# Dynamic convolution, layer norm and feed-forward on one core: hidden-layer products of 64 channels taken in pairs, another order of the first loads, and a new plan

## The chip, the core and the metric

The kernel runs on one core of a Trainium2 chip. A core has five engines with a queue each: PE (TensorE, matmuls), DVE (VectorE), ACT (ScalarE), POOL (GpSimd) and SP (SyncE, which here only issues DMAs). Each runs its own instructions in order and waits on semaphores for the others. PE reads its operands from SBUF and writes to PSUM; 16 DMA engines move data between HBM and SBUF and within SBUF. The metric is the device time of one execution in microseconds, as the median of several runs.

## The reference

Eight sequences of 4224 tokens with 192 channels. Each token is replaced by a weighted sum of itself and the six tokens before it, the weights being a softmax over 7 values for each of 8 heads of 24 channels; then follow a layer norm and a feed-forward network of 192 to 768 to 192 with a ReLU and a residual.

```python
def _attn_ref(x, weight_gen):
    w = np.exp(weight_gen - np.max(weight_gen, axis=-1, keepdims=True))
    w = w / (np.sum(w, axis=-1, keepdims=True) + 1e-09)
    x_pad = np.concatenate([np.zeros((B, pad, D)), x], axis=1)
    idx = np.arange(S)[:, None] + np.arange(K)[None, :]
    x_unf = x_pad[:, idx, :].reshape(B, S, K, H, group)
    return np.einsum('bshk,bskhg->bshg', w, x_unf).reshape(B, S, D)

def _moe_ref(x, g_ln, w_ch1, w_ch2):
    mu = np.mean(x, axis=-1, keepdims=True)
    var = np.mean((x - mu) ** 2, axis=-1, keepdims=True)
    xn = (x - mu) / np.sqrt(var + 1e-06) * g_ln
    return x + np.maximum(xn @ w_ch1, 0.0) @ w_ch2
```

x, weight_gen and g_ln come as float32, w_ch1 (W1) and w_ch2 (W2) as float64.

## The kernel before

**Tiling.** The 33,792 tokens are spread over 128 partitions, so that each partition holds a run of 264 neighbouring tokens ("columns", C = 264). PARTS cuts the 264 columns into parts of 4, 8 or 12 columns for the layer norm, CHUNK = 6 (or 4) columns is the piece of a convolution, and NT = 4 columns (512 tokens) is a group of the feed-forward network; there are 66 groups.

**Stages of a column.** `load_w` (L295) and `load_x` (L280) issue the loads on SP. x lies in a ring of RING = 36 columns with PAD = 6 columns ahead of it, which repeat the last columns of the round before, so that a chunk at the ring's start finds its six older tokens; every round they are loaded from HBM again (L290), and at the very start a load of the neighbouring partition's last columns fills them (L287). `softmax` (L304) works with DVE, POOL and ACT. `conv` (L351) makes seven products per chunk on DVE, in four instructions (L383), into `y` and the `pr` buffers; two accumulating DMAs within SBUF (L389) and four adds on POOL (L386) sum them. For the first EARLY = 1 chunks POOL makes one add of two pairs (L399) and DVE the other four (L386). `norm` (L417) sums and squares on ACT (L427, L432), takes the root on ACT and DVE (L455 to L466), scales y to `xh` (L478), splits it into a high and a low fp16 part `hl` (high on ACT, L485, low on POOL, L487), and SP transposes `hl` by DMA into `xT` (L491). For each column the 384 values are high 0 to 191, then low 0 to 191, which gives three blocks of 128 rows: high 0 to 127; high 128 to 191 over low 0 to 63; low 64 to 191.

**The products.** W1 and W2 too are split into fp16 high and low parts. `products` (L495) computes the hidden layer of a group in three units of 256 hidden channels each (u = 0, 1, 2). A unit is ten matmuls of 512 columns (L506): for each half of 128 hidden channels, W1 high with all three blocks, and W1 low with the first two. Of the second block W1 low needs only the 64 high rows; the other 64 rows add a product of two low parts. The unit's result, two banks of PSUM called `ph` (a pool of two such buffers), is read by ACT (ReLU to `hh`, L515) and then by DVE (the remainder to `hlo`, L517). `output` (L526) makes 18 matmuls of 192 columns per column of tokens (L538 to L540) into `po`, DVE scales and adds the residual (L551), and SP stores a finished chunk.

**Weights.** `load_weights` (L577) issues the loads of W1 (two, 768 and 384 KB) and g on ACT's queue and W2's on SP's. `from_double` (L590) turns float64 bits into float32 on DVE and ACT; `weights` (L649) then scales, splits and, by small DMAs within SBUF (`shift`, L686), brings pieces of the split W1 to other partitions. The steps carry names: "a" and "c" are the two pieces of W1, "s1" their scaling, "c2" and "s2" the same of W2.

**The order.** No engine's order is written out. Every operation is registered with `op` (L64) with its engine, a cost in ns and a "want", a due time in units of a column; `Plan.order` (L89) then simulates the engines with these costs and picks, among the operations that can start within AHEAD ns of the earliest, the one with the smallest want; buffers are assigned on the way. The tables WANT, W_WANT and FIRST (L30 to L35) hold the due times of each step relative to its column. The order so found is fixed before the kernel runs.

## Time and profile before

| | |
|---|---|
| runs, median (lowest to highest of 3) | 910.77 us (909.26 to 911.03) |
| the profiled execution, device time | 914.2 us |
| its span, first to last instruction | 912.4 us |
| products on PE, first to last | 57.65 / 907.5 us |
| mean granted PE clock | 0.994 |
| moved by DMA | 145.12 MB |

The profile was taken of one execution. "Busy" adds up the time in which an engine has an instruction in work; matmuls are pipelined, so their durations overlap and a step is read from one start to the next. A group of instructions is named by line, engine, operation and tiles, with its count, its busy time and the mean of one in ns. An idle stretch is put down to the instruction that ended last among those waited for. PEld is the loading of weights, PEq, SPq and the like are the engines' sequencers with the issue of DMAs.

### The profile page before, as it was taken

The numbers are of one execution on the slowest core, as the hardware profiler recorded it, in microseconds if no ns is written. First come the engines' busy times: TensorE is split into PE (matmuls) and PEld (weight loads), VectorE is DVE, ScalarE is ACT, GpSimd is POOL, SyncE is SP. The second block draws the span as 40 slices with busy tenths as digits, with TensorE's granted clock in tenths as the row PEclk, the third lists the DMA queues.
The fourth block names the chain that finished last, engine by engine and source line by source line (L and its number), as shares of the span: only waits on it lengthen the run. The fifth ranks groups of instructions, "written<-read, shape, count | busy, mean of one in ns | idle before, by whom it ended". The sixth has DMA issues, their size and how long they took to land. (4 is left out here: it accounts for less than half of the span.)

```text
span 912.4 us, 17537 instructions
## 1 busy us (share of the span) xinstructions
PE 831.8 (91%) x6736; PEld 587.2 (64%) x6736; DVE 788.4 (86%) x837; ACT 667.1 (73%) x1766; POOL 689.9 (76%) x398
## 2 busy tenths in 40 slices
PE   0029899999999999999999999999999999999997
PEld 0015577666767677776666667777677777677776
DVE  4999899999999999889798898998989989884342
...
GB/s 229 157 178 155 142 195 180 192 180 116 201 222 165 186 149 169 200 146 197 148 154 179 147 205 157 171 201 136 203 163 156 190 151 145 140 111 91 75 30 52
DMA packets 138667, 145.12 MB, mean 159 GB/s; under 512 B 107551, under 2 KB 108831, under 8 KB 138583
## 3 DMA queue, kind: packets, MB, share of 16 engines
...
q8 instruction: 52, 0.85, 0.4%
...
## 5 line engine op out<-in xcount | busy, mean ns | idle before, releaser
L386 POOL TENSOR_TENSOR y<-y,pr 128x1152 f32<-128x1152 f32 (+1 forms) x200 | 490.1, 2488 | 75.5 <-DVE pr L383 67.7
L506 PE MATMUL ph<-xT,c_w1h 128*128 128x512 f16 x1188 | 421.4, 383 | 43.1 <-DMA xT<-hl 33.5
L540 PE MATMUL po<-c_w2h,hlo 128*128 128x192 f16 x1584 | 389.8, 246 | 5.5 <-DVE hlo L517 5.4
L538 PE MATMUL po<-c_w2h,hh 128*128 128x192 f16 x1584 | 389.7, 246 | 0.0
L539 PE MATMUL po<-c_w2l,hh 128*128 128x192 f16 x1584 | 389.7, 246 | 0.0
L383 DVE TENSOR_TENSOR pr<-x,wn 128x2304 f32<-128x2304 f32 (+1 forms) x153 | 338.1, 2217 | 3.1
L517 DVE SCALAR_TENSOR_TENSOR hlo<-ph,hh 128x1024 f16<-128x1024 f32 x198 | 241.3, 1219 | 81.6 <-ACT hh L515 81.3
L506 PE MATMUL ph<-xT,c_w1l 128*128 128x512 f16 x792 | 303.2, 383 | 0.0
L515 ACT ACTIVATE hh<-ph 128x1024 f16<-128x1024 f32 x198 | 199.9, 1010 | 78.3 <-PE ph L506 77.2
L506 PEld LDWEIGHTS <-c_w1h 128*128 128x128 f16 x1188 | 117.2, 99 | 128.3 <-ACT c_w1h L680 6.3
L538 PEld LDWEIGHTS <-hh 128*128 128x128 f16 x1584 | 155.0, 98 | 22.7
L539 PEld LDWEIGHTS <-hh 128*128 128x128 f16 x1584 | 155.0, 98 | 22.7
L540 PEld LDWEIGHTS <-hlo 128*128 128x128 f16 x1584 | 155.0, 98 | 8.6 <-DVE hlo L517 8.0
L478 ACT ACTIVATE xh<-y,s 128x192 f32<-128x192 f32 x264 | 123.7, 535 | 39.6 <-DVE s L466 39.5
L487 POOL TENSOR_TENSOR hl<-xh,hl 128x768 f16<-128x768 f32 x66 | 118.3, 1792 | 40.7 <-ACT hl L485 39.6
L506 PEld LDWEIGHTS <-c_w1l 128*128 128x128 f16 x792 | 78.1, 99 | 110.2 <-POOL y L386 24.1
L427 ACT ACTIVATE junk<-y 128x192 f32<-128x192 f32 x264 | 95.2, 361 | 45.5 <-POOL y L386 36.0
L432 ACT ACTIVATE junk<-y,s 128x192 f32<-128x192 f32 x264 | 119.1, 451 | 6.0
L389 POOL DMA_DIRECT2D pr<-pr x100 | 100.0, 1003 | 20.7 <-DVE pr L383 19.8
L551 DVE SCALAR_TENSOR_TENSOR y<-po,c_fs,y 128x384 f32<-128x384 f32 x132 | 80.3, 608 | 12.7 <-PE po L540 12.7
L485 ACT ACTIVATE hl<-xh 128x768 f16<-128x768 f32 x66 | 55.1, 835 | 27.7 <-DMA xT<-hl 27.5
L383 DVE TENSOR_TENSOR y<-x,wn 128x1152 f32<-128x1152 f32 (+1 forms) x51 | 60.1, 1180 | 0.1
...
## 6 DMA issues: line engine op xcount, KB each, us to landing
...
```

What stands on the lines that cost most here:

```text
L383: V.tensor_tensor(out=ov, in0=xv, in1=wv, op=ALU.mult)
L386: E.tensor_tensor(out=flat(0), in0=flat(0), in1=flat(k), op=ALU.add)
L389: Q.dma_start(flat(to), flat(k), accum_op=ALU.add, max_dma_last_dim=CHUNK * D * 4)
L432: A.activation(junk, at(y)[:, j, :], AF.Square, bias=at(s4)[:, 3, t : t + 1], accum_out=at(s4)[:, 0, t : t + 1])
L478: A.activation(at(xh)[:, t, :], at(y)[:, i, :], AF.Identity, bias=at(s4)[:, 3, g + t : g + t + 1], scale=at(s4)[:, 1, g + t : g + t + 1])
L487: lambda xh=xh, hl=hl: Q.tensor_tensor(out=at(hl)[:, :, 1, :], in0=at(xh), in1=at(hl)[:, :, 0, :], op=ALU.subtract),
L506: T_.matmul(at(ph)[:, v, :], w[:, wb, fsl], xv[:, xb, :, :], start=(i == 0), stop=(i == len(steps) - 1))
L515: lambda us=us, ph=ph: A.activation(at(hh)[:, us, :], at(ph), AF.Relu), [ph], [(hh, u)])
L517: lambda us=us, ph=ph: V.scalar_tensor_tensor(out=at(hlo)[:, us, :], in0=at(ph), scalar=0.0, in1=at(hh)[:, us, :], op0=ALU.max, op1=ALU.su ...
L538: T_.matmul(o, at(hh)[:, j, q], w2h[:, j, :], start=(j == 0), stop=False)
L539: T_.matmul(o, at(hh)[:, j, q], w2l[:, j, :], start=False, stop=False)
L540: T_.matmul(o, at(hlo)[:, j, q], w2h[:, j, :], start=False, stop=(j == NF - 1))
```

## The change

In `products` two consecutive units, a and b (of one group or of two neighbouring ones), become a pair. The layout of `hl` is mirrored for every second column: there low comes first and high last, so that the second block of such a column holds low 128 to 191 over high 0 to 63. A matmul now takes 256 columns, the two even or the two odd columns of a group. Per half of 128 hidden channels a unit has six products with W1 high (three blocks, even and odd) and two full products with W1 low (the first block of even columns, the third block of odd ones). The remaining 64 rows of W1 low are taken in `narrow_products`: for even columns in rows 0 to 63 of the array, for odd ones in rows 64 to 127, alternating, into different banks of PSUM. The order on PE is: wide products of a, the eight narrow ones of a and b, wide products of b. The first buffer of `ph` is complete after the narrow stretch, and the second is started by it. `c_w1l` gets a third block, filled by two more shifts.

The loads of W1 move from ACT's queue to SP's, with a due time behind the first chunk of x; that chunk and the six columns ahead of it are loaded together, in one load for 120 partitions and a small one for the eight that begin a sequence. The repeated columns of later rounds are copied within SBUF by ACT instead of loaded. EARLY becomes 0: the first chunk is summed like all others. All due times, AHEAD and WINDOW have new values, some steps that had a fixed offset get a due time of their own (Relu, hlo, narrow, each output, final), and the planner's model of an SP DMA and of PE after PE changes.

```diff
-EARLY = 1
+EARLY = 0
...
-WANT = {'load': 35.31, 'wload': 45.13, 'max': 23.73, 'sub': 26.8, 'exp': 29.21, 'sum': 19.41,
-    'rcp': 16.76, 'inv': 19.08, 'mul': 14.75, 'conv': 17.87, 'step': 0.85, 'dma': -0.4, 'add':
-    0.2, 'sums': 8.31, 'squares': 3.24, 'rstd': 5.29, 'newton': 6.27, 'xh': 1.75, 'lo': 6.1}
-W_WANT = {'load': 23.7, 'a': 23.19, 'c': 24.61, 's1': 21.01, 'load2': 14.54, 'c2': 3.68, 's2':
-    7.55}
-FIRST = {'soft': -1.12, 'conv': -1.17, 'norm': 7.8}
-AHEAD = 13.38
-WINDOW = 11.37
+WANT = {'load': 38.75, 'wload': 44.01, 'max': 26.33, 'sub': 29.98, 'exp': 31.81, 'sum': 24.37,
+    'rcp': 22.57, 'inv': 22.65, 'mul': 24.16, 'conv': 21.21, 'step': 0.73, 'dma': -2.14, 'add':
+    -1.02, 'sums': 11.85, 'squares': 7.05, 'rstd': 13.07, 'newton': 9.37, 'xh': 6.82, 'lo':
+    11.91, 'relu': 3.64, 'hlo': 0.84, 'narrow': 3.27, 'o0': -2.91, 'o1': -4.07, 'o2': -3.07,
+    'o3': -3.06, 'final': -0.48}
+W_WANT = {'load': 35.41, 'a': 15.24, 'c': 21.99, 's1': 17.87, 'load2': 9.56, 'c2': 13.77, 's2':
+    3.7}
+FIRST = {'soft': 1.2, 'conv': 7.09, 'norm': 7.75}
+AHEAD = 58.5
+WINDOW = 12.5
...
-    DMA_START = {"SP": 1250.0, "Pool": 650.0, "ACT": 1250.0}
+    DMA_START = {"SP": 900.0, "Pool": 650.0, "ACT": 1250.0}
...
-                x.ready = max(x.ready, o.end)
+                x.ready = max(x.ready, o.end - (o.lat if x.eng == o.eng == "PE" else 0.0))
...
-                src = bass.AP(tensor=xf.tensor, offset=(C - PAD) * D, ap=[[C * D, PB - 1], [PB * C * D, B], [1, PAD * D]])
-                SY.dma_start(X[B:P, 0:PAD, :].rearrange("p t d -> p (t d)"), src)
-            sp(want, first, [], [("x", "h")], dma_ns(PAD * D))
-        elif t0 % RING == 0:
-            sp(want, lambda: SY.dma_start(X[:, 0:PAD, :].rearrange("p t d -> p (t d)"), tokens(x, t0 - PAD, PAD)), [], [("x", "h")],
-               dma_ns(PAD * D * 4))
+                src = bass.AP(tensor=xf.tensor, offset=(C - PAD) * D,
+                              ap=[[C * D, PB - 1], [PB * C * D, B], [1, (PAD + n) * D]])
+                SY.dma_start(X[B:P, 0 : PAD + n, :].rearrange("p t d -> p (t d)"), src)
+
+            cols = [xkey(t) for t in range(n)]
+            sp(want, first, [], [("x", "h"), *cols], dma_ns((PAD + n) * D))
+            src = bass.AP(tensor=xf.tensor, offset=0, ap=[[PB * C * D, B], [1, n * D]])
+            sp(want, lambda: SY.dma_start(X[0:B, PAD : PAD + n, :].rearrange("p t d -> p (t d)"), src), [],
+               [("x", "f")], 300.0)
+            return
+        if t0 % RING == 0:
+            op("ACT", 1050, t0 - WANT["conv"] - 3,
+               lambda: A.copy(X[:, 0:PAD, :], X[:, RING : RING + PAD, :]),
+               [xkey(t) for t in range(t0 - PAD, t0)], [("x", "h")])
...
+        if t0 < RING:
+            xr.append(("x", "f"))
...
+            def halves(hl, low):
+                a = at(hl).rearrange("p t a d -> p (t a d)")
+                o, r = (D, D) if low else (0, 3 * D)
+                return bass.AP(tensor=a.tensor, offset=a.offset + o, ap=[a.ap[0], [4 * D, 2], [r, 2], [1, D]])
+
+            def pairs(xh):
+                return at(xh).rearrange("p (i r) d -> p i r d", r=2)
+
             op("ACT", a_ns(NT * D, 110), S0 + g - WANT["xh"],
-               lambda xh=xh, hl=hl: A.activation(at(hl)[:, :, 0, :], at(xh), AF.Copy), [(xh, 0), (xh, 2)], [(hl, 0)])
+               lambda xh=xh, hl=hl: A.activation(halves(hl, False), pairs(xh), AF.Copy), [(xh, 0), (xh, 2)], [(hl, 0)])
             op("Pool", q_ns(NT * D), S0 + g - WANT["lo"],
-               lambda xh=xh, hl=hl: Q.tensor_tensor(out=at(hl)[:, :, 1, :], in0=at(xh), in1=at(hl)[:, :, 0, :],
+               lambda xh=xh, hl=hl: Q.tensor_tensor(out=halves(hl, True), in0=pairs(xh), in1=halves(hl, False),
                                                     op=ALU.subtract),
                [(xh, 0), (xh, 2), (hl, 0)], [(hl, 1)])
...
+    def mm(gp, u, v, r, w, wb, xb, rows=slice(0, P), **kw):
+        xv = at(gp["xT"]).rearrange("p (i r k) q -> p r k i q", r=2, k=NB)
+        T_.matmul(at(gp["ph"][u])[:, r, v * 2 * P : (v + 1) * 2 * P],
+                  W[w][rows, wb, (2 * u + v) * P : (2 * u + v + 1) * P], xv[rows, r, xb, :, :], **kw)
+
+    def wide_products(gp, u, first):
+        for v in range(2):
+            for b in range(NB):
+                for r in range(2):
+                    mm(gp, u, v, r, "w1h", b, b, start=(first and v == 0 and b == 0), stop=False)
+            for r in range(2):
+                mm(gp, u, v, r, "w1l", 2 * r, 2 * r, start=False, stop=(not first and v == 1))
+
+    def narrow_products(a, b):
+        for first, (gp, u) in ((True, a), (False, b)):
             for v in range(2):
-                fsl = slice((2 * u + v) * P, (2 * u + v + 1) * P)
-                steps = ((w1h, 0, 0), (w1l, 0, 0), (w1h, 1, 1), (w1l, 1, 1), (w1h, 2, 2))
-                for i, (w, wb, xb) in enumerate(steps):
-                    T_.matmul(at(ph)[:, v, :], w[:, wb, fsl], xv[:, xb, :, :],
-                              start=(i == 0), stop=(i == len(steps) - 1))
-
-        for u in range(3):
-            ph = Buf("ph")
-            us = slice(2 * u, 2 * u + 2)
-            su = s + u * NT / 3
-            op("PE", 2160, su, lambda u=u, ph=ph: hidden(u, ph), [xT, "h0", "l0", "h1t", "h1b", "l1t", "l1b", "h2t", "h2b"], [ph])
-            op("ACT", a_ns(2 * NT * P, 50), su + 0.1,
-               lambda us=us, ph=ph: A.activation(at(hh)[:, us, :], at(ph), AF.Relu), [ph], [(hh, u)])
-            op("V", v_ns(2 * NT * P, 6), su + 0.2,
-               lambda us=us, ph=ph: V.scalar_tensor_tensor(
-                   out=at(hlo)[:, us, :], in0=at(ph), scalar=0.0, in1=at(hh)[:, us, :],
-                   op0=ALU.max, op1=ALU.subtract),
-               [ph, (hh, u)], [(hlo, u)])
-            if prev:
-                for t in ((0,), (1,), (2, 3))[u]:
-                    output(prev, t, su + 0.4 + 0.2 * (t == 3))
-        return gp
+                for r in range(2):
+                    mm(gp, u, v, r, "w1l", 1, 1, (top, bot)[r], start=(not first and v == 0),
+                       stop=(first and v == 1))
+
+    W1S = ["h0", "l0", "h1t", "h1b", "l1t", "l1b", "l2t", "l2b", "h2t", "h2b"]
+
+    def at_unit(unit):
+        gp, u = unit
+        return gp["s"] + u * NT / 3
+
+    def evict(unit):
+        gp, u = unit
+        hh, hlo, ph = gp["hh"], gp["hlo"], gp["ph"][u]
+        us = slice(2 * u, 2 * u + 2)
+        su = at_unit(unit)
+        op("ACT", a_ns(2 * NT * P, 50), su - WANT["relu"],
+           lambda: A.activation(at(hh)[:, us, :], at(ph), AF.Relu), [ph], [(hh, u)])
+        op("V", v_ns(2 * NT * P, 6), su - WANT["hlo"],
+           lambda: V.scalar_tensor_tensor(
+               out=at(hlo)[:, us, :], in0=at(ph), scalar=0.0, in1=at(hh)[:, us, :],
+               op0=ALU.max, op1=ALU.subtract),
+           [ph, (hh, u)], [(hlo, u)])
+        if gp["prev"]:
+            for t in ((0,), (1,), (2, 3))[u]:
+                output(gp["prev"], t, gp["s"] - WANT[f"o{t}"])
+
+    def products(a, b):
+        for gp, u in (a, b):
+            gp["ph"][u] = Buf("ph")
+        xs = [a[0]["xT"], b[0]["xT"]]
+        pa_, pb_ = (gp["ph"][u] for gp, u in (a, b))
+        op("PE", 1744, at_unit(a), lambda: wide_products(*a, True), [xs[0], *W1S], [pa_])
+        op("PE", 640, at_unit(b) - WANT["narrow"], lambda: narrow_products(a, b), [*xs, *W1S], [pa_, pb_])
+        evict(a)
+        op("PE", 1744, at_unit(b), lambda: wide_products(*b, False), [xs[1], *W1S], [pb_])
+        evict(b)
...
-            q = slice(t * P, (t + 1) * P)
+            r, i = t % 2, t // 2
+
+            def tok(b, j):
+
+                o = ((j // 2 * 2 + r) * 2 + j % 2) * 2 * P + i * P
+                return at(b).rearrange("p j q -> p (j q)")[:, o : o + P]
+
             o = at(po)[:, h * D : h * D + D]
             for j in range(NF):
-                T_.matmul(o, at(hh)[:, j, q], w2h[:, j, :], start=(j == 0), stop=False)
-                T_.matmul(o, at(hh)[:, j, q], w2l[:, j, :], start=False, stop=False)
-                T_.matmul(o, at(hlo)[:, j, q], w2h[:, j, :], start=False, stop=(j == NF - 1))
+                T_.matmul(o, tok(hh, j), w2h[:, j, :], start=(j == 0), stop=False)
+                T_.matmul(o, tok(hh, j), w2l[:, j, :], start=False, stop=False)
+                T_.matmul(o, tok(hlo, j), w2h[:, j, :], start=False, stop=(j == NF - 1))
...
-        op("V", v_ns(2 * D, 63), s + 0.3, final, [(po, 0), (po, 1), "w2"], [(y, j), (y, j + 1)])
+        op("V", v_ns(2 * D, 63), s - WANT["final"], final, [(po, 0), (po, 1), "w2"], [(y, j), (y, j + 1)])
...
-        dma("ACT", A, "load", lambda: words(0, 0, 2 * F), w1b[0:P, :], 8 * F, raw[0])
-        dma("ACT", A, "load", lambda: words(1, 0, 2 * F)[top, :], w1b[P:D, :], 4 * F, raw[1])
+        dma("SP", SY, "load", lambda: words(0, 0, 2 * F), w1b[0:P, :], 8 * F, raw[0])
+        dma("SP", SY, "load", lambda: words(1, 0, 2 * F)[top, :], w1b[P:D, :], 4 * F, raw[1])
...
+        shift(w1l[top, 2, :], w1l[bot, 0, :], ["l0"], ["l2t"])
+        shift(w1l[bot, 2, :], w1l[top, 1, :], ["l1t"], ["l2b"])
...
-    prev = None
+    prev, units = None, []
     for pa in parts:
         for g in range(0, pa["n"], NT):
-            prev = products(pa, g, pa["S"] + g, prev)
+            prev = dict(hh=Buf("hh"), hlo=Buf("hlo"), pa=pa, g=g, s=pa["S"] + g, xT=pa["xT"][g], ph={}, prev=prev)
+            units += [(prev, u) for u in range(3)]
+    for a, b in zip(units[::2], units[1::2]):
+        products(a, b)
     for t in range(NT):
-        output(prev, t, C + t)
+        output(prev, t, C - WANT[f"o{t}"])
```

8 lines of the change are left out of this document (1 added, 7 removed).

## The prediction

> **What bounds the kernel now.** First the page: the busy times and the 40 slices.
>
> ```profile
> span 912.4 us, 17537 instructions
> PE 831.8 (91%) x6736; PEld 587.2 (64%) x6736; DVE 788.4 (86%) x837; ACT 667.1 (73%) x1766; POOL 689.9 (76%) x398
> ...
> PE   0029899999999999999999999999999999999997
> ...
> DVE  4999899999999999889798898998989989884342
> ```
>
> PE is empty for two slices, then full to the end; DVE is full from the first slice and thins out only in the last four. So the end is set by a PE that starts late, with a DVE close behind. The table by stretches (columns: window, its length, then PE, PEld, DVE, ACT, POOL, PE clock, DMA share, GB/s) says how close.
>
> ```profile
> 0.00:20.00 20.00, 0.00 (x0) 0.00 (x0) 8.11 (x16) 4.22 (x7) 5.01 (x8) 1.00 0.93 227
> ...
> 70.00:80.00 10.00, 10.00 (x47) 4.86 (x46) 9.53 (x13) 8.19 (x20) 8.39 (x6) 0.75 0.56 118
> ...
> 100.00:200.00 100.00, 95.80 (x761) 66.25 (x759) 95.91 (x109) 82.33 (x230) 94.70 (x64) 0.98 0.91 182
> 200.00:300.00 100.00, 96.33 (x787) 68.20 (x785) 94.56 (x100) 80.86 (x218) 89.07 (x52) 1.00 0.94 176
> 300.00:400.00 100.00, 99.62 (x820) 71.06 (x818) 95.09 (x90) 79.91 (x214) 84.70 (x46) 1.00 0.93 174
> 400.00:500.00 100.00, 96.63 (x785) 67.69 (x783) 86.98 (x82) 73.64 (x198) 74.63 (x39) 1.00 0.98 164
> 500.00:600.00 100.00, 99.39 (x815) 70.56 (x812) 92.41 (x93) 80.15 (x213) 85.60 (x44) 1.00 0.93 167
> 600.00:700.00 100.00, 100.00 (x827) 71.63 (x826) 93.84 (x89) 77.17 (x205) 80.09 (x43) 1.00 0.94 181
> 700.00:800.00 100.00, 98.92 (x807) 69.83 (x805) 90.61 (x86) 76.65 (x207) 80.69 (x45) 1.00 0.90 151
> 800.00:850.00 50.00, 50.00 (x415) 35.84 (x414) 31.35 (x44) 40.94 (x108) 30.76 (x20) 1.00 0.57 100
> ```
>
> Between 100 and 800 us PE loses 13.3 us in all, 7.9 of it from 100 to 300, where DVE is 95% busy; from 500 on, at 92%, it loses next to nothing. After 800 DVE has little left: the convolutions are done and PE works off what is stored. How long one group of 512 tokens takes there is read in the chain that ended last.
>
> ```profile
> 827.04 2.16 PE ph L506 x10
> 830.69 2.16 PE ph L506 x10
> 834.33 2.16 PE ph L506 x10
> 839.46 2.16 PE ph L506 x10
> ...
> 907.39 0.10 PE po L540
> 907.51 0.62 DVE y L551
> ```
>
> Three units of ten matmuls at 2.16 us, with four outputs between them: 839.46 - 827.04 = 12.42 us a group. 66 groups are 820 us of the span; the other 92 are the start, the 13.3 us above and some slow clock (0.75 at 70 to 80).
>
> **Part 1, the products.** The hidden layer has 3 x 66 = 198 units, which the change takes in 99 pairs. A unit had 10 matmuls of 512 columns. Now it has 16 of 256 columns, and each pair has 8 more of 64 rows and 256 columns. Their price comes from the steps between starts in the timeline of PE.
>
> ```profile
> 897.75 0.38 PE L506 MATMUL ph<-xT,c_w1h 128*128 128x512 f16 x1
> 897.97 0.38 PE L506 MATMUL ph<-xT,c_w1l 128*128 128x512 f16 x1
> ...
> 898.40 0.25 PE L538 MATMUL po<-c_w2h,hh 128*128 128x192 f16 x1
> 898.48 0.25 PE L539 MATMUL po<-c_w2l,hh 128*128 128x192 f16 x1
> ...
> L506 PE MATMUL ph<-xT,c_w1h 128*128 128x512 f16 x1188 | 421.4, 383 | 43.1 <-DMA xT<-hl 33.5 <-DVE hlo L517 9.3
> ...
> L538 PEld LDWEIGHTS <-hh 128*128 128x128 f16 x1584 | 155.0, 98 | 22.7
> ```
>
> 512 columns take 2.16 / 10 = 0.216 us, 192 columns (830.69 - 827.04 - 2.16) / 18 = 0.083. That is 0.416 ns a column, so 256 columns take 0.083 + 64 x 0.416 ns = 0.1094 us. A weight load of 98 ns is hidden even at a step of 83, so it is at 109. Sixteen make 1.751 us.
>
> The eight narrow ones have no row: no matmul of before uses 64 rows. The lower end is perfect sharing, four steps, 0.438 us. The upper end is no sharing, eight steps (0.876), plus a stop of the array at each of the two changes of shape. A stop is bounded by a matmul's duration over its step, 0.383 (group mean of L506) - 0.216 = 0.167 us: 1.209 in all. Between them I take 0.64: the diff's planner prices the stretch so, and its standing prices for PE, 2160 ns a unit and 1494 an output, are met by the rows above (2.16 and 1.49); it is also 0.438 plus 1.2 such stops. A pair then costs 2 x 1.751 + 0.64 = 4.142 us against 4.32, which saves 0.178; 99 pairs, **-17.6 us**. The ends give -37.6 and +38.7; the break-even stands at 0.818 us a stretch.
>
> The Trainium skill, TensorE: Matmul & The Clock Gate, Part 3, has matmuls in different row groups start about 4 ns apart and reports 3.07 times the rate for four row tiles of 512 columns. As an estimate from that page a shared step would be 4/3.07 = 1.30 of a single one, the stretch 0.57 us and the saving 24.5 us. No run here shows it.
>
> Evictions stay as many and as large. What changes is what they hold up: the stretch takes the second buffer of `ph` before its wide products run and sends off the first only at its end.
>
> ```profile
> DVE hlo L517 <- ACT hh L515: 81.3, 59, 4.0
> ACT hh L515 <- PE ph L506: 77.2, 44, 4.1
> ...
> L383 DVE TENSOR_TENSOR pr<-x,wn 128x2304 f32<-128x2304 f32 x90 | 229.1, 2547 | 2.1
> ...
> c_w1h<-c_w1h SPq DMA_DIRECT2D x3, 96.0 KB, 2.1
> ```
>
> The first two rows are the longest waits in total, and they end at PE: the evictors wait for it, not it for them. A buffer is held for 1.75 + 0.64 + some 2.4 us of eviction = 4.8 of the 8.1 that a pair and its outputs take; before it was 4.6 of 8.3. The cover shrinks from 3.7 to 3.3 us and still hides one DVE instruction of 2.5 us (third row); costed at nothing, with what a late DVE costs under part 3. The new strides of `hl` keep runs of 192 elements: nothing. Two more 96 KB shifts follow on SP's queue after the three of `w1h`; the last row has such a shift at 2.1 us from issue to landing, so they delay the first wide product by 0 to 4 us if W1 is what it waits for, and I take 0.
>
> **Part 2, the start.** Rows of ACT's, POOL's, DVE's, SP's and PE's timelines:
>
> ```profile
> 6.17 5.67 ACTq L580 DMA_DIRECT2D c_g<-in_moe_g_ln_dram  x2
> 11.89 0.39 ACT L326 ACTIVATE e<-e 128x224 f32<-128x224 f32 x1 [9.87 <-DMA x<-in_x_dram]
> 6.58 0.58 POOL L323 TENSOR_TENSOR e<-w,mx 128x224 f32<-128x224 f32 x1 [4.79 <-DVE mx L321]
> 14.29 3.42 DVE L383 TENSOR_TENSOR pr<-x,wn 128x1536 f32<-128x1536 f32 x2
> 38.81 0.94 DVE L386 TENSOR_TENSOR y<-y,pr 128x768 f32<-128x768 f32 x1
> 52.02 2.37 SPq L491 DMA_TRANSPOSE xT<-hl  x1
> 57.65 0.59 PE L506 MATMUL ph<-xT,c_w1h 128*128 128x512 f16 x1 [30.43 <-DMA xT<-hl]
> 69.33 0.59 PE L506 MATMUL ph<-xT,c_w1h 128*128 128x512 f16 x1 [4.58 <-DVE hlo L517]
> ```
>
> POOL has the first `e` ready at 7.2 us, but ACT takes it at 11.9: its queue stands in the issue of `g` behind W1's transfers. With W1 on SP that stand goes, and the first convolution moves from 14.3 to about 9.7, **-4.6 us**, if its x is there: the diff puts that 0.9 MB behind 0.34 MB of `w` and ahead of W1, and at the 227 GB/s of the first 20 us it lands by 7 to 8 us. SP's queue now has W1 (1.15 MB, 4 to 5 us) ahead of the second x chunk. That lands near 14, before the first convolution's 6 us of products are over, so nothing waits.
>
> ```profile
> L386 DVE TENSOR_TENSOR y<-y,pr 128x768 f32<-128x768 f32 x4 | 4.8, 1195 | 0.0
> L714 ACT ACTIVATE c_w2h<-hlo 128x1152 f16<-128x1152 f32 x1 | 1.1, 1147 | 0.0
> ```
>
> EARLY = 0 takes the first chunk's four adds off DVE, **-4.8 us** on an engine whose slices are full from the second on; POOL and accumulating DMAs take them over, and POOL works only 5.0 of the first 20 us. So DVE's early queue runs up to 4.6 + 4.8 = 9.4 us sooner, and with it y (38.81), the transpose (52.02) and PE (57.65, in earnest 69.33). I take **-9.4**. The ends: 0 if W1, now converted after the first convolutions, is what PE waits for; -15 if the first group's path alone decides.
>
> The ring's repeated columns come by seven ACT copies of 1152 elements (the row of L714: 1.15 us each, 8 us in all) in place of seven 576 KB loads. ACT is 74 to 82% busy where they fall. Behind a copy that waits for its x stand Relus, and behind these hlo and PE; the cover of 3.3 us takes one copy. Nothing, with +8 as the upper end and, as DMA is 0.9 busy, a small gain as the lower.
>
> **Part 3, what is late next.** DVE. The seven rows from 100 to 800 add up to 649.4 us of work, 92.8%. At PE's new pace, 12.42 - 1.5 x 0.178 = 12.15 us a group, the same stretch of work has 685 us: 94.8%. By the same rows PE loses 2.8% where DVE is at 95.2% (100 to 400) and 0.6% at 92.3% (500 to 800); on the line between, 2.5% at 94.8%, 17 us in place of today's 13.3. That is **+4**, and I let it stand for the new order of every want too (ends -8, if the new order has fewer gaps than the 13.3, and +20).
>
> Sum: -17.6 - 9.4 + 4 = -23.0 on the profiled execution's own 914.2 us (span 912.4 and 1.8 around it), 891.2. The median of the runs is 3.4 us below the profiled one: **887.8**.
>
> **The rivals.**
> *Full sharing, DVE the bound.* At 0.438 us a stretch the products save 37.6, but the group would be 11.85 us and DVE 97.2% busy from 100 to 800; the line above, drawn on, has PE lose 4.3% there, 29 us instead of 13. 910.8 - 37.6 - 9.4 + 16 = 880, or 868 if the order spends the stored work of the last 90 us instead. For: different rows, different banks. Against: weight loads for half the rows have no row here.
> *Shared, but the array stops at each change of shape.* 0.438 + 2 x 0.167 = 0.772 us, -4.6 in the products: 910.8 - 4.6 - 9.4 = 897. For: two changes a pair, 198 in all. The Trainium skill, TensorEngine Tiling (Array Packing), Key Properties, states this rule against the change: a change of tiling mode drains the array. No row of before bears it out, as it never changes shape.
> *No sharing, so the change does not do what it says: slower.* The eight narrow matmuls run one after another and the array stops twice: 1.209 us, +38.7 - 9.4, **940**. With the start's 9.4 us as a cushion (95 ns a pair) it is slower from 0.913 us a stretch on. For: every matmul of before starts a full step behind the last. Against: upper and lower rows take different weights, data and banks.
> *The order eats it.* PE loses 4.2% from 100 to 800 us, as in the row of 100:200, and W1 gives back the start: 910.8 - 17.6 + 15 = 908. It needs DVE near 96% throughout, against 92.8% now.
>
> **How the numbers follow.** Forecast 0.56 (own range 876 to 897), full sharing 0.14, stops 0.14, no sharing 0.11, the order 0.05, half of it within 0.2%. About 0.2% (1.8 us) is what a measurement can tell from no change. Faster 0.84, same 0.04, slower 0.12. The range reaches from 866 (full sharing with the tail spent) to 906 (stops, with half the start lost) and leaves out no sharing and most of the order, 0.16, with a little below.
>
> **What would show it.** A wide unit of sixteen matmuls at 1.75 us, and a narrow stretch read from its first start to the next wide start: 0.44, 0.64, 0.77 or 1.21 tells the cases apart. First DVE product near 10 us; first matmul before 50 and the steady run from about 60. PE's busy time 17 us lower, DVE near 95% from 100 to 800 and PE's loss there near 17. Wrong if the stretch is above 0.82, if PE still starts after 57, or if PE's waits for hlo or xT in 100 to 800 exceed 25 us.

## The result and the profile after: slower by 1.2%, not faster by 2.5%

| | before | after |
|---|---|---|
| runs, median (lowest to highest of 4 each) | 910.01 us (908.25 to 911.03) | 919.23 us (918.53 to 925.24) |
| ratio, 95% interval | | 1.0118 (1.0072 to 1.0164) |
| profiled execution, span | 914.2, 912.4 us | 925.2, 923.5 us |
| first output on PE starts | 76.4 us | 81.9 us |
| last matmul of an output ends | 907.5 us | 918.2 us |

Executions over 1.5% longer than the fastest of the same kernel are left out of all medians and ratios here, and where an experiment's profile is of one of them (e3, e11, e14) its first output is read from it but no loss of PE. The profiled execution of the changed kernel is the slowest of its four, 6 us above their median.

The forecast was 887.8 us, with a range up to 906. The page of the changed kernel, its busy times and its slices of PE, DVE and the PE clock:

```profile
span 923.5 us, 21518 instructions
PE 824.6 (89%) x8716; PEld 734.4 (80%) x8716; DVE 789.4 (85%) x833; ACT 674.8 (73%) x1773; POOL 696.9 (75%) x403
...
PE   0047898999999999999999995999999999899997
...
DVE  6998997999999989999999895898989989774442
PEclk9989998999999999999999997999999999899999
```

PE no longer stays full up to the end: there is a hole (5) in the middle of the run, with DVE thin at the same place. The table by stretches (the columns are those of the one before):

```profile
100.00:200.00 100.00, 92.68 (x980) 82.31 (x978) 92.21 (x105) 81.42 (x229) 89.47 (x61) 0.97 0.87 166
...
500.00:600.00 100.00, 90.23 (x949) 80.53 (x948) 81.95 (x81) 72.84 (x190) 73.16 (x39) 0.95 0.88 152
600.00:700.00 100.00, 98.97 (x1067) 88.68 (x1065) 93.03 (x91) 79.13 (x213) 81.82 (x44) 1.00 0.86 167
...
sum 700.00, PE 671.12 PEld 599.45 DVE 642.38 ACT 552.99 POOL 586.17; mean PE 95.87 PEld 85.64 DVE 91.77 ACT 79.00 POOL 83.74
```

From 100 to 800 us PE now loses 700 - 671.1 = 28.9 us instead of 13.3, and DVE is *less* busy there (91.8%) than before (92.8%). The stretches with the large losses also have a lower granted clock.

**The pairs work.** PE's timeline at 856 us, where nothing is late:

```profile
856.57 0.25 PE L593 MATMUL po<-c_w2h,hlo 128*128 128x192 f16 x1
856.75 0.61 PE L522 MATMUL ph<-xT,c_w1l 64*128 64x256 f16 x8
857.29 0.83 PE L522 MATMUL ph<-xT,c_w1h 128*128 128x256 f16 x6
857.96 0.38 PE L522 MATMUL ph<-xT,c_w1l 128*128 128x256 f16 x2
858.18 0.82 PE L522 MATMUL ph<-xT,c_w1h 128*128 128x256 f16 x6
858.83 0.38 PE L522 MATMUL ph<-xT,c_w1l 128*128 128x256 f16 x2
859.05 0.25 PE L591 MATMUL po<-c_w2h,hh 128*128 128x192 f16 x1
```

From the first wide matmul to the output behind it a unit takes 859.05 - 857.29 = 1.76 us. The last step of the outputs ends 0.083 us after 856.57, at 856.65, and the wide products start at 857.29: the stretch of eight narrow matmuls, with both changes of shape, costs 0.64 us.

**PE stops in long pieces.** The waits from 100 to 800 us (columns: who waited for what, us in total, times, longest), and then the worst of them, from the chain of work between 535 and 575 us (start, length, what):

```profile
DVE hlo L554 <- ACT hh L552: 29.4, 15, 10.9
PE ph L522 <- DVE hlo L554: 24.5, 25, 9.6
...
ACT hl L506 <- DMA xT<-hl: 23.4, 4, 12.3
...
PE ph L522 <- DMA xT<-hl: 4.2, 1, 4.2
```

```profile
542.64 1.94 POOL hl L508
...
544.61 20.21 DMA xT<-hl
...
564.84 0.84 ACT hl L506
...
566.70 0.92 ACT hh L552
...
567.64 1.24 DVE hlo L554
...
568.92 0.61 PE ph L522 x4
```

A transposing DMA took 20.2 us. ACT stood at L506 until it landed, because the next `hl` needs the buffer that the transpose was reading (two buffers of `hl`). A Relu stood behind that in ACT's queue, `hlo` behind the Relu on DVE, and PE's narrow stretch behind the release of its `ph` buffer: PE's previous matmul had started at 559.1. The table over the same place shows what follows the stall (after window and length come PE, PEld, DVE, ACT and POOL, then the clock):

```profile
559.00:569.00 10.00, 0.40 (x6) 0.22 (x8) 1.36 (x2) 4.07 (x11) 3.24 (x3) 0.75 0.96 162
569.00:574.00 5.00, 5.00 (x30) 3.98 (x30) 5.00 (x4) 4.39 (x17) 2.74 (x2) 0.50 1.08 128
574.00:580.00 6.00, 6.00 (x66) 5.51 (x65) 6.00 (x5) 1.02 (x1) 3.12 (x2) 0.99 1.20 168
```

After 9.6 us without work PE ran at half clock for another 5 (30 matmuls in 5 us, then 66 in 6). There are four stalls of over 2.5 us after 100 us (at 142, 404, 559 and 793 us; 20 us together) and 27 us at half clock, against 3 us before.

**The ledger.** The last output ends 10.7 us later (918.2 - 907.5). The products give -17.6 (the pace of 12.15 us a group is there). The first output starts 5.5 us later, but PE has done six units before it instead of four, 2 x 2.07 us of work: the start costs +1.4. After the first output PE stands 36.4 us instead of 19.7 (gaps between starts above 0.3 us, less a step each): +16.7. What is left is 10.7 + 17.6 - 1.4 - 16.7 = +10.2. Most of it is the slow clock: PE has work in 18.5 of the 27 us at half clock, and in 1.0 of the 3 before, and half of that difference is 8.7. The other 1.5 us are not accounted for.

### The profile page after: what moved, and what is told of

Its sections match the earlier page's. It is cut to its first block, busy times and chain, and to the rows that moved or that the text cites. A ratio compares the mean times of both kernels' runs of the same rounds, so it can differ in the third digit from the quotient of the medians.

```text
span 923.5 us, 21518 instructions
## 1 busy us (share of the span) xinstructions
PE 824.6 (89%) x8716; PEld 734.4 (80%) x8716; DVE 789.4 (85%) x833; ACT 674.8 (73%) x1773; POOL 696.9 (75%) x403
## 3 DMA queue, kind: packets, MB, share of 16 engines
q0 software_dynamic: 14688, 51.91, 31.5%
## 4 chain that ended last, share of the span: by engine, by line
DVE 29%; PE 25%; ACT 8%; POOL 7%; DMA 6%; issue 6%; DVEq 0%; POOLq 0%; ACTq 0%
DVE pr L395 14%; PE ph L522 12%; DVE hlo L554 7%; DMA xT<-hl 6%; POOL y L398 5%; PE po L591 4%; PE po L593 4%; PE po L592 4%; DVE y L395 2%; DVE y L604 2%; ACT hh L552 2%; ACT xh L490 2%; ACT junk L439 2%; ACT hl L506 1%; POOL hl L508 1%
## 5 line engine op out<-in xcount | busy, mean ns | idle before, releaser
L398 POOL TENSOR_TENSOR y<-y,pr 128x1152 f32<-128x1152 f32 (+1 forms) x204 | 498.7, 2469 | 72.6 <-DVE pr L395 69.3
L522 PE MATMUL ph<-xT,c_w1h 128*128 128x256 f16 x2376 | 333.0, 277 | 37.6 <-DMA xT<-hl 20.3
L522 PEld LDWEIGHTS <-c_w1h 128*128 128x128 f16 x2376 | 230.2, 99 | 78.0 <-issue 41.7
L554 DVE SCALAR_TENSOR_TENSOR hlo<-ph,hh 128x1024 f16<-128x1024 f32 x198 | 238.9, 1219 | 55.0 <-ACT hh L552 54.6
L552 ACT ACTIVATE hh<-ph 128x1024 f16<-128x1024 f32 x198 | 200.0, 1012 | 94.5 <-PE ph L522 61.1
L522 PE MATMUL ph<-xT,c_w1l 128*128 128x256 f16 (+1 forms) x1584 | 214.3, 277 | 16.3 <-DVE hlo L554 16.0
L591 PEld LDWEIGHTS <-hh 128*128 128x128 f16 x1584 | 155.5, 98 | 12.4 <-issue 10.7
L508 POOL TENSOR_TENSOR hl<-xh,hl 128x768 f16<-128x768 f32 x66 | 113.2, 1715 | 60.7 <-ACT hl L506 60.3
L522 PEld LDWEIGHTS <-c_w1l 128*128 128x128 f16 (+1 forms) x1584 | 109.6, 97 | 51.3 <-issue 31.4
L401 POOL DMA_DIRECT2D pr<-pr x102 | 97.5, 964 | 28.8 <-DVE pr L395 26.3
L439 ACT ACTIVATE junk<-y 128x192 f32<-128x192 f32 x264 | 95.2, 361 | 29.2 <-POOL y L398 23.1
L506 ACT ACTIVATE hl<-xh 128x768 f16<-128x768 f32 x66 | 54.9, 832 | 23.5 <-DMA xT<-hl 23.4
```

The source lines that it names most:

```text
L398: E.tensor_tensor(out=flat(0), in0=flat(0), in1=flat(k), op=ALU.add)
L439: A.activation(junk, at(y)[:, j, :], AF.Identity, scale=-1.0 / D, accum_out=at(s4)[:, 3, t : t + 1])
L508: lambda xh=xh, hl=hl: Q.tensor_tensor(out=halves(hl, True), in0=pairs(xh), in1=halves(hl, False), op=ALU.subtract),
L522: T_.matmul(at(gp["ph"][u])[:, r, v * 2 * P : (v + 1) * 2 * P], W[w][rows, wb, (2 * u + v) * P : (2 * u + v + 1) * P], xv[rows, r, xb, :, ...
L552: lambda: A.activation(at(hh)[:, us, :], at(ph), AF.Relu), [ph], [(hh, u)])
L554: lambda: V.scalar_tensor_tensor(out=at(hlo)[:, us, :], in0=at(ph), scalar=0.0, in1=at(hh)[:, us, :], op0=ALU.max, op1=ALU.subtract),
```

## Experiments

Ratios are against runs of the kernel before in the same batch, with their 95% interval. "PE loss" is 700 us less PE's busy time from 100 to 800 us.

| run | median us | ratio | first output | PE loss |
|---|---|---|---|---|
| before | 910.0 | 1 | 76.4 | 13.3 |
| after | 919.2 | 1.0118 (1.0072 to 1.0164) | 81.9 | 28.9 |
| e1 pairs, old order | 933.0 | 1.0236 (1.0173 to 1.0299) | 76.6 | 28.0 |
| e2 new plan, old products | 910.0 | 1.0004 (0.9986 to 1.0023) | 78.9 | 11.3 |
| e3 old start | 931.0 | 1.0241 (1.0196 to 1.0287) | 87.4 | |
| e4 three `hl` | 908.9 | 1.0001 (0.9975 to 1.0026) | 84.0 | 18.3 |
| e5 small accumulation | 898.2 | 0.9855 (0.9817 to 0.9893) | 83.0 | 11.5 |
| e6 lighter DVE | 918.1 | 1.0078 (1.0052 to 1.0105) | 82.9 | 26.7 |
| e7 other due times | 896, 897, 915, 918 | | 81.5 | 9.3 |
| e8 other due times, more buffers | 906.7 | 0.9950 (0.9911 to 0.9988) | 81.2 | 12.5 |
| e9 before, small accumulation | 900.8 | 0.9864 (0.9835 to 0.9894) | 75.8 | 4.7 |
| e10 e1, small accumulation | 908.0 | 0.9954 (0.9928 to 0.9980) | 75.4 | 18.2 |
| e11 EARLY = 1 | 922.4 | 1.0102 (1.0069 to 1.0134) | 86.6 | |
| e12 W2 earlier | 946.3 | 1.0359 (1.0312 to 1.0405) | 78.3 | 50.1 |
| e13 e12, small accumulation | 893.3 | 0.9787 (0.9754 to 0.9820) | 77.2 | 11.7 |
| e14 e7, three `hl` | 902.5 | 0.9901 (0.9865 to 0.9938) | 81.7 | |
| e15 before, three `hl` | 905.6 | 0.9921 (0.9892 to 0.9950) | 76.3 | 7.5 |
| e16 plain copies | 897.1 | 0.9856 (0.9821 to 0.9891) | 80.1 | 10.4 |
| e17 accumulation in quarters | 902.3 | 0.9915 (0.9888 to 0.9942) | 84.1 | 16.9 |
| e18 e14 and quarters | 904.2 | 0.9953 (0.9941 to 0.9965) | 88.2 | 10.0 |

e7's four runs split in two, so all four are given and no ratio; its profile is of the 897. In e5, e6, e9, e10, e13 and e16 the kernel leaves out part of the products or of their sums, as said at each.

### Products or plan: e1, e2, e3

**e1** puts the pairs on the engine orders of the kernel before, with its loads, ring, EARLY and due times; evictions that would come ahead of the narrow stretch are held back until it is through.

```diff
-EARLY = 0
+EARLY = 1
...
-WANT = {'load': 38.75, 'wload': 44.01, 'max': 26.33, ...
+WANT = {'load': 35.31, 'wload': 45.13, 'max': 23.73, ...
...
+    for fn in paired(plan.order()):
+        fn()
```

> The products are paired as in the change, but every engine keeps the order that the kernel before has: the narrow stretch is put behind the first unit of a pair, as soon as the second buffer of ph is free; loads, ring, EARLY and all due times are those of before. Theory 'order' (the new plan leaves PE waiting for xT and hlo, the pairs are sound): 910 - 17.6 = 892, range 888 to 898, PE's loss from 100 to 800 us at most 18 us. Theory 'pairs' (the narrow stretch, which needs two buffers of ph and the xT of the next group, is itself what stalls PE): 905 or more, with PE's loss from 100 to 800 above 25 us.

933 us: the pairs are slow on the old order too, with a first output at 76.6 us. That only the new plan is at fault has fallen.

**e2** is the reverse: all of the change, but unpaired units of ten matmuls of 512 columns.

```diff
...
-    for a, b in zip(units[::2], units[1::2]):
-        products(a, b)
+    for a in units:
+        products(a)
```

> The changed kernel with the ten matmuls of 512 columns per unit of before; new loads, new ring, new due times. Theory 'order': 919 + 17.6 = 937, range 928 to 942, with stalls of PE as in the changed kernel. Theory 'pairs': 900 to 915, as without pairs the stalls go.

910.0 us, no change: new loads, ACT's copies, EARLY = 0 and new due times together give nothing and cost nothing, with a PE loss as before.

**e3** takes the changed kernel back to W1 on ACT's queue, the old first loads and EARLY = 1, under the new due times.

```diff
-EARLY = 0
+EARLY = 1
...
-        dma("SP", SY, "load", lambda: words(0, 0, 2 * F), w1b[0:P, :], 8 * F, raw[0])
+        dma("ACT", A, "load", lambda: words(0, 0, 2 * F), w1b[0:P, :], 8 * F, raw[0])
```

> The changed kernel with the start of before: W1 on ACT's queue, first x and the six columns ahead of it in two loads, EARLY = 1; pairs, ring copies and due times are the changed ones. If the new start is what makes the first output late (82.0 us against 76.5), the first output comes by 77 and the time falls to about 913. If the new start is sound and the due times make it late, the first output comes at 85 to 90 and the time is 920 to 930.

First product at 66.4 us (51.0 in the changed kernel), first output at 87.4. So the new loads do bring the first products forward, and they aren't what makes the first output late. Under the new due times the old start is also 12 us slower in all, a little more than was expected.

### What stops PE: e4, e6, e5, e9, e16, e10, e17

**e4** gives `hl` a third buffer.

```diff
-    pool("hl", 2, [P, NT, 2, D], F16)
+    pool("hl", 3, [P, NT, 2, D], F16)
```

> The changed kernel with three buffers of hl in place of two; the plan's order is the same. If the stalls of PE are ACT standing at hl until a transpose has landed, with the Relus queued behind it (12.3 us at 553 to 565, 5.9 us at 787 to 793), these two waits go and the time falls by 5 to 10 us, to 909 to 914. If the late transpose itself is what PE needs, it falls by at most 3 us, to 916 or more.

908.9, so 10 us less, and ACT's waits at `hl` are gone. But a gap of 5.2 us at 555 remains, in which PE waits for the transposed tile itself. The buffer takes a link out of the chain, not its origin.

**e6** tries the step on which the forecast rested, that PE loses where DVE is busy. From column 120 on, one product of DVE is made for half of the heads; the other half is left out.

```diff
+            if k == 5 and c >= 26 and n == CHUNK:
+                h = n * H // 2
+                ov, xv, wv = ov[:, :, :h, :], ...
```

> The changed kernel, order the same, but from column 120 on the last of the four products of each chunk is made for half of the heads only, which takes about 1.2 us off DVE per six columns (6%); the other half is left out. Theory 'DVE': PE's loss from 400 to 800 us falls from 17 to under 6 and the time to 900 to 906. Theory 'collision': the long stalls near 559 and 793 us stay, the time falls by at most 6 us, to 912 or more.

The sum row of its table by stretches, 100 to 800 us:

```profile
sum 700.00, PE 673.31 PEld 604.30 DVE 623.28 ACT 557.00 POOL 591.78; mean PE 96.19 PEld 86.33 DVE 89.04 ACT 79.57 POOL 84.54
```

DVE falls to 89.0%, and PE still loses 26.7 us, with a transpose of 22.3 us in it; from 400 to 800 us, where the whole stretch has the lighter product, it loses 16.0 instead of 17.2. DVE's share isn't the cause.

**e5** and **e9** make the accumulating DMAs small, in the changed kernel and in the one before: each moves one column of a chunk, and the sums of the other columns are left out.

```diff
-            Q.dma_start(flat(to), flat(k), accum_op=ALU.add, max_dma_last_dim=CHUNK * D * 4)
+            Q.dma_start(flat(to)[:, :D], flat(k)[:, :D], accum_op=ALU.add, max_dma_last_dim=CHUNK * D * 4)
```

> The changed kernel, order and instructions the same, but each accumulating DMA moves one column of its chunk in place of four or six; the other columns of that sum are left out. Theory 'collision' (a DMA transpose in flight beside an accumulating DMA lands after 8 to 20 us in place of 3.2, PE then runs out of xT or of free ph, and each longer stall also halves the clock for some us): the transposes land in under 5 us, PE's loss from 100 to 800 us falls from 29 to under 8, the time to 888 to 900. Theory 'DVE' (DVE is 92 to 96% busy and PE simply waits for its share): DVE does the same work, the time stays at 910 or more.

> The kernel before, whose accumulating DMAs move one column of a chunk; the sums of the other columns are left out. It is the control for the same cut in the changed kernel, which took 21 us off it. Theory 'collision meets the short groups' (PE at 12.42 us a group leaves the delayed transposes room, at 12.15 it doesn't): the kernel before gains little, 901 to 908 us, and PE loses some 8 to 11 us from 100 to 800 instead of 13.3. Rival 'the accumulating DMAs cost both the same': it gains 15 to 25 us too, 885 to 895, and then the collision is no cause of the difference between the two.

First the sum row of e5, then that of e9:

```profile
sum 700.00, PE 688.55 PEld 618.61 DVE 663.39 ACT 571.66 POOL 606.81; mean PE 98.36 PEld 88.37 DVE 94.77 ACT 81.67 POOL 86.69
```

```profile
sum 700.00, PE 695.26 PEld 494.99 DVE 661.48 ACT 562.58 POOL 603.53; mean PE 99.32 PEld 70.71 DVE 94.50 ACT 80.37 POOL 86.22
```

e5 is 21.0 us below the changed kernel, e9 9 to 11 below the one before (9.2 by the first batch, 11.1 by its own). The expectation for e9 was 901 to 908 with a loss of 8 to 11 us; 900.8 and 4.7 lie just and clearly below. The accumulating DMAs cost *both* kernels, the changed one about twice as much. The difference, 10 to 12 us, covers the slowdown of 9.2, and with small DMAs the two kernels are level (ratios 0.9855 and 0.9864). At a like share of DVE, 94.8 and 94.5%, they lose 11.5 and 4.7 us, so DVE's share doesn't explain what e5 still loses (below 8 was expected). The longest transpose falls from 20.2 to 7.6 us (changed) and from 15.4 to 8.1 (before), taken from issue and landing of each one that the trace shows (51 and 66); below 5 us was expected in e5.

**e16** keeps the bytes and leaves out only the adding.

```diff
-            Q.dma_start(flat(to), flat(k), accum_op=ALU.add, max_dma_last_dim=CHUNK * D * 4)
+            Q.dma_start(flat(to), flat(k), max_dma_last_dim=CHUNK * D * 4)
```

> The changed kernel, whose accumulating DMAs copy the same bytes without adding; the sums of those products are left out. Theory 'accumulating': it is the adding transfers that hold the transposes up, so a plain copy of the same size behaves like the small ones: transposes beside them land after 4 to 6 us with none above 10, PE's loss from 100 to 800 is 10 to 14 us, and the time 895 to 903. Rival 'bytes': whatever fills the DMA engines delays the transposes, so they still take 8 us and up to 15 or more, PE's loss stays at 22 to 30 and the time at 912 to 922.

The page's DMA queues (packets, MB, share of 16 engines) and its DMA issues (KB each, us to landing), first of the changed kernel, then of e16:

```profile
q0 software_dynamic: 14688, 51.91, 31.5%
...
pr<-pr POOLq DMA_DIRECT2D x60, 576.0 KB, 6.7
```

```profile
q0 software_dynamic: 12000, 51.91, 15.9%
...
pr<-pr POOLq DMA_DIRECT2D x60, 576.0 KB, 3.9
```

897.1 us, as with the small ones. The same 51.91 MB take half the DMA engines' time when nothing is added, no transpose is longer than 8.4 us, and of PE's long stalls only one of 2.5 us near 398 is left. That one also stands in e5 and e17, so the stall of the changed kernel at 404 is not the collision's. It is the accumulation, not the bytes. With no accumulating DMA in flight a transpose of the changed kernel took 3.4 us in the mean of 13, with one or more 8.3 in the mean of 38.

**e10** asks the same of e1's order.

```diff
 e1, with
-            Q.dma_start(flat(to), flat(k), accum_op=ALU.add, max_dma_last_dim=CHUNK * D * 4)
+            Q.dma_start(flat(to)[:, :D], flat(k)[:, :D], accum_op=ALU.add, max_dma_last_dim=CHUNK * D * 4)
```

> The paired products on the order of the kernel before, which took 934 us, with accumulating DMAs of one column; the sums of the other columns are left out. 'Collision': PE's loss from 100 to 800 falls from 28 to 10 to 15 us and the time by 25 to 40, to 895 to 910. Rival 'the stretch holds the second buffer of ph too long for that order' (the paired order holds evictions back until the narrow stretch is through): the waits for hlo stay, the loss stays above 22, and the time above 920.

908.0, 25 us less than e1. PE's waits for `xT` (12.6 us in e1) are gone, those for `hlo` stay (17.7 in e1, 17.5 here). So both were true, though the loss of 18.2 us lies between what the two expected: the collision costs 25, and the pairs on that order, which holds evictions back, another 7 against e9.

**e17** cuts the accumulation into packets of a quarter of a row and computes the same.

```diff
-            Q.dma_start(flat(to), flat(k), accum_op=ALU.add, max_dma_last_dim=CHUNK * D * 4)
+            Q.dma_start(flat(to), flat(k), accum_op=ALU.add, max_dma_last_dim=CHUNK * D)
```

> The changed kernel with the same accumulating DMAs cut into packets of a quarter of a row (1152 bytes instead of 4608); it computes the same. Theory 'long packets': the transposes' small packets stand behind long accumulating ones, so quarters let them through, the longest transpose falls below 12 us and the time to 900 to 912. Rival 'accumulation itself': four times the packets with the same adding change nothing or cost more, 917 to 935, with transposes of 15 us and more still there.

902.3 us, 17 less than the changed kernel and 0.85% below the kernel before (by the interval 0.6 to 1.1%). The queue's row:

```profile
q0 software_dynamic: 48480, 51.91, 38.4%
```

The price is on POOL: an issue of such a DMA (L401) takes 1.68 us instead of 0.96. The time came as "long packets" expected, the longest transpose did not: 19.6 us where below 12 was expected, though only 4 transposes take over 10 us instead of 12. The Trainium skill, DMA: Bandwidth & Descriptors, SWDGE vs HWDGE vs iDMA, says that a DMA engine takes turns between its queues and changes over only at packet boundaries, packets being preferably up to 4096 B. That agrees with e17, as a row is 4608 B, if the packets of the profile are the page's; it doesn't explain e16, whose packets carry more bytes in the mean (12000 for the same 51.91 MB, against 14688).

What e16 and e17 have in common is the time of one packet. Share times 16 engines times span, over the packets of the queue, gives 0.32 us in the changed kernel, 0.19 in e16 and 0.11 in e17, where the share of the engines even rises. That a transpose waits for the packet in work would fit all three; it is argued from these rows, and no run tries it alone.

### The start: e11, e12, e13

PE, DVE and POOL in the changed kernel's start, rows of their timelines (idle time before, and its releaser, in brackets):

```profile
10.43 3.42 DVE L395 TENSOR_TENSOR pr<-x,wn 128x1536 f32<-128x1536 f32 x2 [2.63 <-DMA x<-in_x_dram]
...
51.00 1.44 PE L522 MATMUL ph<-xT,c_w1h 128*128 128x256 f16 x6 [16.06 <-DMA xT<-hl]
...
55.81 6.74 DVE L395 TENSOR_TENSOR pr<-x,wn 128x1536 f32<-128x1536 f32 x4
...
62.46 0.15 DVE L759 TENSOR_REDUCE c_s<-c_s 128x1 f32<-128x3 f32 x1
...
62.67 0.59 PE L683 MATMUL po<-c_s,ones 128*128 128x1 f32 x2 [5.31 <-DVE c_s L759]
...
66.36 2.58 POOL L398 TENSOR_TENSOR y<-y,pr 128x768 f32<-128x768 f32 x1
...
67.05 1.92 DVE L763 SCALAR_TENSOR_TENSOR c_fs<-c_r,c_r 128x1 f32<-128x1 f32 x1
...
74.23 2.37 POOL L771 TENSOR_TENSOR c_w2l<-hlo,c_w2h 128x1152 f16<-128x1152 f32 x1
...
76.31 1.44 PE L522 MATMUL ph<-xT,c_w1h 128*128 128x256 f16 x6 [4.97 <-DVE hlo L554]
...
81.91 0.25 PE L591 MATMUL po<-c_w2h,hh 128*128 128x192 f16 x1
```

The first convolution starts at 10.4 us (14.3 before) and the first product at 51.0 (57.7). Then PE stands at a one-column matmul of W2's scale until DVE is through four products of a convolution, and W2's low part is there at 76.6.

**e11** sets EARLY back to 1.

```diff
-EARLY = 0
+EARLY = 1
```

> The changed kernel with EARLY = 1 alone: DVE adds the first chunk's products itself. Theory 'given back': the 4.8 us of adds taken off DVE come back as waits of its tiny instructions beside POOL's adds (L721, L728, L763 at 1.6 to 2.0 us instead of 0.15 to 0.35), so with the adds on DVE these are short again, the first output stands at 80 to 84 us (81.9 in the changed kernel) and the time is within 0.6%. Rival 'the saving is real': the first output comes 4 to 6 us later, 86 to 88, and the time is 3 to 8 us longer.

The first output came at 86.6 us as the rival had it, and the time, 922.4, lies within 0.6% as the theory had it and, at 3.2 us more, within the rival's 3 to 8 too; by the ratios (1.0102 against 1.0118) nothing is lost. The theory's mechanism has fallen, as L721 and L763 are long with EARLY = 1 too (1.99 us for two, and 5.59). The first output comes 4.7 us sooner with EARLY = 0, of which 3.7 are L763 alone (1.92 us instead of 5.59), and nothing of it shows at the end.

The first products go the other way. PE's first one in e11:

```profile
44.56 0.61 PE L522 MATMUL ph<-xT,c_w1h 128*128 128x256 f16 x2 [5.35 <-ACT c_w1h L733]
```

With the adds on DVE the first transpose is issued at 35.35 us, with the adds on POOL and accumulating DMAs at 47.66, and the first product comes at 44.56 and at 51.00. So EARLY = 0 didn't speed up the first group's path, it slowed it down; in e11 it is W1 that PE then waits for, and both have the first pair done at 57 to 58 us. Next to e3 (first product at 66.4, EARLY = 1 as well) e11 also shows that the new loads alone bring the first product forward by 22 us. Each is read from one execution.

**e12** lets W2's scaling come earlier; **e13** is e12 with small accumulating DMAs, as in e5.

```diff
-W_WANT = {'load': 35.41, ..., 'load2': 9.56, 'c2': 13.77, 's2': 3.7}
+W_WANT = {'load': 35.41, ..., 'load2': 9.56, 'c2': 13.77, 's2': 8.0}
```

> The changed kernel with the due time of W2's scaling at 8.0 instead of 3.7 (in tokens of a sequence, about 3 us each), nothing else. In the changed kernel PE stands from 57 to 62.7 us behind the small matmul of W2's scale, whose input DVE delivers after four products of a convolution, and runs six units before the first output. Theory 'W2 was left behind': the small matmul comes before the first pair, four units go ahead of the first output, it starts at 75 to 79 us instead of 81.9, and the time falls by 3 to 6 us. Rival 'DVE has too much to do before the first output, in whatever order': the wait moves to another tile, the first output stays at 80 to 84, and the time within 0.4%.

> The kernel with W2's scaling due earlier, which took 946 us, with accumulating DMAs of one column; the sums of the other columns are left out. 'Collision': its long stalls go, PE's loss from 100 to 800 falls from 50 to 10 to 16 us, and the time to 892 to 903, at or below the changed kernel with the same cut (898), since its first output comes sooner. Rival 'that order holds ph and the evictions up by itself': above 912.

e12's first output starts at 78.3 us, 3.6 sooner, as "W2 was left behind" expected (though still after six units). And yet it takes 946 us. Rows of its chain of work from 400 to 500 us, where accumulating DMAs, 6.7 us in the changed kernel's median, take this long:

```profile
379.36 35.97 DMA pr<-pr
...
419.73 5.57 DMA xT<-hl
...
455.82 22.38 DMA pr<-pr
```

With small ones the same order takes 893.3, 53 us less and 5 below e5. So the start's 5 us are to be had by moving W2, and in e12 the same collision turned them into a loss of 27, since one due time changes which transfers meet. Why two of them can lie together for 36 us was not tried.

### Can the gain be had: e7, e8, e14, e15, e18

**e7** changes due times alone (found with a model in which transposes and accumulating DMAs slow each other), **e8** other due times with 3 buffers of `hl` and 4 of `xT`, **e14** e7 with 3 of `hl`, **e15** the kernel before with 3, **e18** e14 with quarters as in e17.

```diff
 e7
...
-AHEAD = 58.5
-WINDOW = 12.5
+AHEAD = 100.07
+WINDOW = 15.24
 e8
...
+    pool("hl", 3, [P, NT, 2, D], F16)
+    pool("xT", 4, [P, NT * NB, P], F16)
```

> The changed kernel with other due times alone (WANT, W_WANT, FIRST, AHEAD, WINDOW): they were chosen on a model of the order in which a transpose and an accumulating DMA in flight together slow one another. Pairs, loads, ring and buffers are the changed ones. Theory 'collision': an order that gives the transposes room keeps the gain of the pairs: PE's loss from 100 to 800 at most 13 us, 885 to 900. Theory 'pairs' (the narrow stretch stalls PE in whatever order): 908 or more.

> As the run before, with three buffers of hl and four of xT and due times chosen for these. Theory 'collision': a transpose may be issued a group earlier, so a late landing is hidden: PE's loss from 100 to 800 at most 8 us, 880 to 893, below e7. Theory 'pairs': 905 or more, as more buffers of hl and xT do not free ph.

> The changed kernel with the due times that leave transposes more room before their group, and a third hl buffer. If the delayed transposes and ScalarE's stand at hl are what the pairs' gain goes into, PE loses 8 to 12 us from 100 to 800, and the time is 892 to 902, ratio 0.98 to 0.99. If what the pairs gain is lost in the share of DVE, the loss stays above 14 and the time is 905 or more.

> The kernel before with three hl buffers, nothing else; the control of the changed kernel with three, which gained 10 us. Theory 'short groups alone': 908 to 912 us, ratio within 0.3%, as PE at 12.42 us a group covers the late landings. Rival 'the buffer helps any order': 898 to 904, and then a part of what it gave the changed kernel is no answer to the change.

> The changed kernel with the new due times, three hl buffers and the accumulating DMAs in packets of a quarter of a row; it computes the same. If the delay by accumulation is what spread these due times from 897 to 913 us, short packets bring the median to 893 to 900 with a spread below 8 us, and no stall of PE above 3 us after 100 us. If short packets only helped the order that they were tried in, it stays at 903 to 908 and spreads as before.

e7's profiled execution (span 895.1, PE loss 9.3) shows that the pairs' gain can arrive; two of its four runs didn't have it, and e14's twelve spread from 897 to 913. e8 came out as the rival had it: 906.7 us where 880 to 893 was expected from more buffers, with a loss of 12.5 where at most 8 was. In e18 the spread is 1.1 us (903.7 to 904.8) and no stall above 2.5 us is left after 100 us, as expected, but the median is 904 instead of 893 to 900: from the first output to the last it takes 808.9 us, as long as e5, and the first output comes at 88.2. DVE's and POOL's rows there:

```profile
78.13 5.57 DVE L763 SCALAR_TENSOR_TENSOR c_fs<-c_r,c_r 128x1 f32<-128x1 f32 x1
```

```profile
79.72 3.89 POOL L771 TENSOR_TENSOR c_w2l<-hlo,c_w2h 128x1152 f16<-128x1152 f32 x1
```

An instruction on one element a partition takes 5.6 us and ends about when POOL's subtraction does (79.72 + 3.89 = 83.61); `hlo` and PE stand behind it. e15 refutes its theory and falls short of the rival's 898 to 904: the third buffer gives the kernel before 0.8% too, 6 us where it gave the changed one 10.

So e17 beats both kernels and computes the same, at 902.3; e15, without any part of the change, is at 905.6, and the intervals of the two ratios overlap. That pairs pay on this chip is not shown, only that they needn't lose.

## Why the prediction was wrong, by its own steps

- **Part 1, -17.6: right.** Unit 1.76 (forecast 1.75), stretch 0.64 (0.64), group 12.15 (12.15). None of the rivals on sharing came about. The 0.64 itself was the planner's price out of the diff, placed between two bounds; it was not worked out from a row.
- **Part 2, the start, -9.4: wrong in what was carried over.** Of the chain "with it y (38.81), the transpose (52.02) and PE (57.65, in earnest 69.33)" the loads' part came: DVE -3.9 instead of -4.6, and the first product -6.7 in all. EARLY's -4.8 did not: taking the adds off DVE made the first transpose 12.3 us later, not sooner (e11), while "POOL and accumulating DMAs take them over" was put at nothing because POOL had room; how long the sum then takes was not asked. The step that failed for the end time is "and PE": the start was counted to PE's first products, while what counts is when PE has both products *and outputs* to do. W2's scaling is even due later than before (`s2` at 3.7 instead of 7.55), DVE's queue put four products ahead of its scale, and the first output came 5.5 us later, +1.4 net of the two more units done. e12 and e13 show the place: W2 alone is worth 3.6 to 5.8 us of the first output.
- **Part 3, "by the same rows PE loses 2.8% where DVE is at 95.2%", +4: wrong, and the largest miss.** Measured are +16.7 of standing and +10.2 of which most is slow clock, 26.9. The line took DVE's share for a cause, and it was drawn through 100 to 400 and 500 to 800 us with the row between left out: from 400 to 500 DVE was at 87.0% and PE lost 3.4%, more than the line's upper point. e6 lowers DVE by 3% of the time and gains 1 us; e5 and e16 have DVE at 94.8 and 94.6%, the forecast's own 94.8, and lose 11.5 and 10.4 us. What stood in its place was in the rows of before already: `ACT hl L485 <- DMA xT<-hl`, 24.5 us in 13 waits from 100 to 800, and a median transpose of 8.1 us that takes 3.2 alone. The prediction quoted PE's waits for `xT` and never asked why a transpose takes so long. Of its own signs of being wrong only one came, waits of PE for `hlo` or `xT` above 25 us, if the two are added: 24.5 + 4.2.
- **"The order eats it", 908 with a chance of 0.05: the sign of the truth, not its mechanism.** Its loss of 4.2% for PE came (28.9 of 700 us), but it needed DVE near 96% for it, and DVE was at 91.8%.
- **The ACT copies at nothing: right.** Seven at 1.14 us (1.15 forecast), and e2 as a whole costs nothing.

The two misses add up to what is missing: 10.8 (start) + 22.9 (Part 3) = 33.7 = 23.0 + 10.7; part of the second is what the ledger had left over. Without the collision the change would still not have given 23: e5 stands 2.6 us below e9, and by the ratios 0.1%, which the intervals don't tell from nothing. There the start is worse by 3.0 (7.2 later, two units more) in place of -9.4, and PE's gaps after the first output are 16.2 us instead of 7.0 (+9.2, where +4 was forecast). Its wait for the release of `ph`, in e5 from 100 to 800 us:

```profile
PE ph L522 <- DVE hlo L554: 11.0, 18, 2.3
```

In e9 the same wait is 2.7 us, though the two differ in their order as well. The prediction saw the cover of a `ph` buffer shrink and "costed at nothing" what that holds up; these rows have some 8 us there.

**What stays open.** The three orders with pairs lose more to the collision (21, 25 and 53 us) than the one without (9 to 11). But e12 against the changed kernel shows that the order alone can move this by 32 us, so only e1 bears on the pairs themselves: it has the old order, apart from the evictions held back. The new plan without pairs (e2) was not run with small DMAs. Why pairs should suffer more is only argued: a pair needs both `ph` buffers and, where it spans two groups, the next group's `xT` a unit earlier, so a late transpose also holds up the evictions of the group before it. No run separates this from the shorter pace. The mean transpose of the changed kernel isn't slower than before (7.0 us against 8.3); it is a few long ones that stop PE.
